# A first round of weights decoded over more steps, and the second token tile's first products put ahead of the first tile's second products

## The chip, the cores and the metric

The kernel runs on one core of one Trainium2 chip. The metric is the device time of one execution in microseconds (us); of several executions the median is taken, and lower is better. Engine names in the rows: PE is the matrix engine, PEld its weight loads, DVE the vector engine, ACT the scalar engine, POOL the GpSimd engine, SP the engine that issues most transfers.

## The reference

What is computed is a sliding-window attention followed by two feed-forward layers, all in float32. Batch is 2, heads 8, sequence 768, head size 64; the model width is 512 and the hidden width 2048, so there are 1536 tokens.

```python
scores = scale * np.matmul(q, k.transpose(0, 1, 3, 2))
keep = is_sink | in_window              # 4 sink keys, window of 128 keys
scores = np.where(keep, scores, -1000000000.0)
a = np.exp(scores - np.max(scores, axis=-1, keepdims=True))
a = a / (np.sum(a, axis=-1, keepdims=True) + 1e-09)
x = np.matmul(a, v)                     # then heads side by side: [1536, 512]
...
h = x @ w_in                            # first layer
g = np.where(h > 0.0, h, np.exp(np.minimum(h, 0.0)) - 1.0)
x = g @ w_out
...
h = x @ w_in2                           # second layer
g = np.maximum(h, 0.0) + alpha * np.minimum(h, 0.0)
out = g @ w_out2
```

## The kernel before, in words

**Numbers.** The layer products are made to float32 accuracy out of a reduced float format: each operand is kept as a high part and a low part, and `matmul3` (L287) makes three matmuls for each pair (high by high, high by low, low by high). A *product* below is one call of `Mlp.g1` or `Mlp.g2`: four pairs, so twelve matmuls. `g1` (L303, tiles `h`) multiplies one 128-row block of the first weight matrix by a tile of tokens; its second half `after` makes the activation `u` and splits it into `gh` (ACT) and `gl` (POOL). `g2` (L341, tiles `o`) multiplies four such blocks by the second weight matrix and adds into `acc`.

**Weights.** They arrive as 64-bit words, in *halves* of 128 by 512: `halves(0)` lists the eight of the first round (four row blocks, each an `io=0` half for `g1` and an `io=1` half for `g2`). `load_w` starts the transfer into one of three `raw` buffers. `decode_w` (L257) takes a half apart: two ACT operations (`wx`, `wq`; L266 and L267), four DVE operations (L269 to L278), an ACT copy to the high part `wh` (L282) and a subtraction for the low part `wl` (L284). It is a generator that stops three times, so that its pieces can be laid between other work. Its scratch tiles come from the pool `wdec`, which lives as long as the kernel. The subtraction runs on DVE, or on the engine passed as `sub`.

**Attention steps.** The attention is cut into 32 units; each has one or two blocks of up to 110 queries for two heads. The units of a token tile are done head pair after head pair: units 0 to 3 give the first 220 tokens, 4 to 7 the next 220, 8 to 15 the next 328 (these units have two blocks and one block in turn), and 16 to 31 the second batch in the same way. The loop over `s` (L610), from 0 to 33, is software-pipelined and its order is written by hand (`manual_schedule`, L597). Step `s` makes the scores of unit `s` (`qk` on PE, L510; mask and minimum on DVE, L518; exponential and its sum on ACT, L523), the values product of unit `s-2` (`x`, L575; its high part `xh` on ACT, its low part `xl` on DVE), the normalisation of unit `s` (`st` on DVE, then `s` on POOL, L540) and the transposes of unit `s-1` (`t` on PE, L554, copied out to `pt`, L638). Each engine executes its own instructions in the order in which they stand.

**Filling.** From step 5 on one product of the first layer's first round is put into each step (`fill`, L588 to L594): for each token tile first its four `g1`, then its four `g2`. When eight or more are due (`FILL_MAX`, L62), a second one is put into the same step. In steps 0 to 4 dummy matmuls (`keep_busy`) stand in the products' place. In steps 0 to 7 one half of the first round is decoded in each step (L625 to L629, L652 to L654); the subtraction of the last four halves is on POOL.

**After the steps.** `mlp_rounds` (L393) does the fifth token tile of the first round, and then all other rounds in tiles of 512 tokens; the halves of the next round are decoded between the products. There the order on each engine is the scheduler's, not written by hand, and it may put an instruction anywhere ahead where its buffers are free. The pools of the attention steps are closed before (`inner.close()`, L669), and the next round's weight pool `wb` takes their memory.

Of the kernel before, what the change touches and what calls it, by code (L numbers as in the profile page):

```python
# [21 lines left out]
P = 128  # L22
# [12 lines left out]
HP = H // 2  # L35
# [19 lines left out]
MS = {2: 0, 3: 1, 4: 5}  # L55
# [6 lines left out]
FILL_MAX = 8  # L62
# [49 lines left out]
def attention_mlp2(  # L112
# [20 lines left out]
    wdec = ctx.enter_context(tc.tile_pool(name="wdec", bufs=2))  # L133
# [123 lines left out]
    def decode_w(pool, m, fc, io, sub=None):  # L257
# [26 lines left out]
        (sub or nc.vector).tensor_tensor(out=wl, in0=xf, in1=wh, op=ALU.subtract)  # L284
# [10 lines left out]
    class Mlp:  # L295
# [3 lines left out]
        def __init__(self, gp, ps):  # L299
            self.gp, self.ps = gp, ps  # L300
            self.g = {}

        def g1(self, m, c0, n, fc):  # L303
# [12 lines left out]
            def after():  # L316
                u = tmp.tile([P, big], F32, tag="u", name=f"u{m}_{t}_{fc}")[:, :n]
                gh = self.gp.tile([P, big], F32R, tag="gh", name=f"gh{m}_{t}_{fc}")[:, :n]
                gl = self.gp.tile([P, big], F32R, tag="gl", name=f"gl{m}_{t}_{fc}")[:, :n]
# [73 lines left out]
    def mlp_rounds(mlp, items, wpools):  # L393
# [22 lines left out]
        def weights_step():  # L416
            j = state["at"]
            if j + 2 < len(order):
                load_w(*order[j + 2][1:])
            done(decode_w(*order[j]))  # L420
            state["at"] = j + 1
# [24 lines left out]
    def distance(blk):  # L446

        rel = relp.tile([P, KW[blk]], I32, tag=f"rel{blk}", name=f"rel{blk}")
# [29 lines left out]
    relp = ctx.enter_context(tc.tile_pool(name="relp", bufs=1))  # L478
    rels = {blk: distance(blk) for blk in MASKS}
# [4 lines left out]
    def fast_path():  # L484
# [4 lines left out]
        ga = inner.enter_context(tc.tile_pool(name="ga", bufs=FG + 1))  # L489
        at = inner.enter_context(tc.tile_pool(name="at", bufs=2))  # L490
        mlp = Mlp(ga, ps)
        soft, trans = {}, {}
        wraw.update(wfirst)

# [96 lines left out]
        for c0, n, t in TOK0[:-1]:  # L591
            at_ = last_of[t * HP + HP - 1] + 2
            fill += [(at_, lambda c0=c0, n=n, fc=fc: mlp.g1(0, c0, n, fc)) for fc in range(FG)]
            fill += [(at_, lambda c0=c0, n=n, d=d: mlp.g2(0, c0, n, 0, d)) for d in range(KC)]  # L594


        order = inner.enter_context(tc.manual_schedule())  # L597
# [3 lines left out]
        for j in range(WPRE, WPRE + 3):  # L601
            load_w(*ws[j])
            if j < HP:
                load_v(j)
        for g in range(HP, HP + LB):
            load_kq(g, at)
            load_v(g, at)
        decodes = {}
        gates = []
        for s in range(nu + 2):  # L610
# [44 lines left out]
            if WPRE <= s and s + 3 < len(ws):  # L655
                load_w(*ws[s + 3])
# [15 lines left out]
        mlp.gp = gb  # L672
        rounds = [(k, t) for k in range(1, 2 * NR) for t in TOK]
        mlp_rounds(mlp, [(0, TOK0[-1])] + rounds, (wa, wb))
        outer.close()

    def general_path():

        with ExitStack() as outer:
            ps = outer.enter_context(tc.tile_pool(name="gps", bufs=4, space=PSUM))  # L680
            wraw.update(wfirst)
            for h in halves(0):
                if h not in wraw:
                    load_w(*h)
                done(decode_w(wa, *h))
# [71 lines left out]
            mlp_rounds(mlp, [(k, t) for k in range(2 * NR) for t in TOK], (wa, wb))  # L757
# [58 lines left out]
```

## Time and profile before

| what | value |
| --- | --- |
| device time, median of 3 runs | 672.32 us (671.1 to 672.47) |
| device time of the profiled execution | 673.24 us |
| its span | 671.1 us |
| PE busy | 642.0 us (96%) |
| DVE busy | 440.8 us (66%) |
| ACT busy | 316.5 us (47%) |
| POOL busy | 207.9 us (31%) |
| mean granted clock of PE | 0.983 of full speed |

The span is the time from the first to the last recorded instruction; the device time has about 2 us more around it. The busy shares are means over the whole span. The attention steps take about the first 180 us of it; the rest is the rounds of the two layers. A timeline row gives the start in us, the length in us, the engine, the source line, the operation, output and input tiles with their sizes, how many instructions were merged, and in brackets the idle time before it on that engine with what ended it.

### The profile page before, as it was taken

How to read it: one execution, taken by the hardware profiler on the slowest of the kernel's cores; microseconds unless marked ns; L12 is line 12 of the kernel's file. 1: busy time of each engine (PE TensorE's matmuls, PEld its weight loads, DVE VectorE, ACT ScalarE, POOL GpSimd, SP SyncE). 2: the span in 40 equal slices, each digit the busy share in tenths (PEclk: the TensorE clock that was granted, in tenths of full speed). 3: DMA queues.
4: the chain of work that ended last, by engine and by line, in shares of the span. 5: the costliest groups of instructions: out<-in, count | busy, mean ns of one | idle time of the engine just before them, and what ended most of it. 6: DMA issues, size and time to landing. Idle time of an engine off the chain costs nothing.

```text
span 671.1 us, 9665 instructions
## 1 busy us (share of the span) xinstructions
PE 642.0 (96%) x3444; PEld 527.0 (79%) x3444; DVE 440.8 (66%) x925; ACT 316.5 (47%) x717; POOL 207.9 (31%) x257
## 2 busy tenths in 40 slices
PE   7966999999999899999999999999999999999996
PEld 6745888888877677888888888888888888888885
DVE  5798566756499997668465876694559673343332
ACT  5676476656478685547445733453524230110010
POOL 2346244534123322133205453332123311331130
PEclk8898899999999999999999999999999999999999
DMA  8665324620044242121112211221111000000112
GB/s 266 169 165 182 106 58 122 170 79 25 1 154 133 91 156 95 49 77 63 63 54 72 64 63 52 75 67 61 63 63 63 32 0 1 1 0 1 63 46 85
DMA packets 21659, 52.87 MB, mean 79 GB/s; under 512 B 2658, under 2 KB 9826, under 8 KB 21602
## 3 DMA queue, kind: packets, MB, share of 16 engines
q1 hardware_dynamic: 21024, 51.93, 24.8%
q8 instruction: 29, 0.48, 0.3%
q10 hardware_dynamic: 578, 0.24, 0.2%
q14 instruction: 28, 0.23, 0.1%
HBM read 49.01 MB, written 3.15 MB: 78 GB/s over the span
## 4 chain that ended last, share of the span: by engine, by line
PE 80%; DVE 11%; ACT 4%; issue 3%; POOL 1%; DMA 1%; ACTq 0%; DVEq 0%; POOLq 0%; SPq 0%
PE o L292 37%; PE h L292 34%; PE x L575 3%; PE t L554 2%; PE qk L510 2%; DVE wx L275 2%; ACT s L523 2%; DVE wl L284 1%; DVE wx L269 1%; DVE wx L278 1%; PE busy L250 1%; DVE u L323 1%; DVE pt L638 1%; DVE wx L272 1%; ACT wx L266 1%
## 5 line engine op out<-in xcount | busy, mean ns | idle before, releaser
L336 POOL TENSOR_TENSOR gl<-u,gh 128x512 fp32r<-128x512 f32 (+3 forms) x104 | 131.5, 1264 | 341.6 <-ACT gh L335 307.2
L292 PE MATMUL o<-gh,wh 128*128 128x512 f32 (+3 forms) x416 | 159.2, 383 | 3.7 <-DVE u L323 2.0
L292 PE MATMUL h<-xh,wh 128*128 128x512 f32 (+3 forms) x416 | 158.9, 382 | 0.0
L292 PE MATMUL o<-gl,wh 128*128 128x512 f32 (+3 forms) x416 | 157.2, 378 | 0.8 <-POOL gl L336 0.8
L292 PE MATMUL h<-xl,wh 128*128 128x512 f32 (+3 forms) x416 | 157.1, 378 | 0.0
L292 PE MATMUL h<-xh,wl 128*128 128x512 f32 (+3 forms) x416 | 156.9, 377 | 0.0
L292 PE MATMUL o<-gh,wl 128*128 128x512 f32 (+3 forms) x416 | 156.5, 377 | 0.0
L335 ACT CAST gh<-u 128x512 fp32r<-128x512 f32 (+3 forms) x104 | 61.0, 586 | 140.9 <-DVE u L331 118.9
L357 DVE TENSOR_TENSOR acc<-o,acc 128x512 f32<-128x512 f32 x72 | 49.4, 688 | 76.9 <-PE o L292 76.9
L292 PEld LDWEIGHTS o<-gh,wh 128*128 128x128 f32 x416 | 78.5, 189 | 23.2 <-DVE u L323 4.1
L292 PEld LDWEIGHTS h<-xh,wh 128*128 128x128 f32 x416 | 78.6, 189 | 17.1 <-DVE u L323 0.3
L292 PEld LDWEIGHTS o<-gl,wh 128*128 128x128 f32 x416 | 78.8, 189 | 15.9 <-POOL gl L336 1.8
L292 PEld LDWEIGHTS h<-xl,wh 128*128 128x128 f32 x416 | 78.7, 189 | 14.6
L292 PEld LDWEIGHTS h<-xh,wl 128*128 128x128 f32 x416 | 78.6, 189 | 14.7
L292 PEld LDWEIGHTS o<-gh,wl 128*128 128x128 f32 x416 | 78.7, 189 | 14.5
L540 POOL TENSOR_SCALAR s<-s,st 110x250 f32<-110x250 f32 (+5 forms) x112 | 52.7, 488 | 86.0 <-DVE st L536 42.6
L282 ACT CAST wh<-wx 128x512 fp32r<-128x512 f32 x64 | 39.5, 619 | 67.7 <-DVE wx L278 29.4
L327 DVE TENSOR_SCALAR u<-h,alpha_sb 128x512 f32<-128x512 f32 x48 | 35.9, 748 | 48.4 <-PE h L292 48.3
L523 ACT ACTIVATE s<-s,st 110x250 f32<-110x250 f32 (+5 forms) x112 | 53.1, 476 | 20.8 <-DVE st L518 20.8
L278 DVE CUSTOM_DVE_ANT_0 wx<-wx,wq 128x1024 uint16<-128x1024 uint16 x64 | 58.0, 906 | 1.3
L284 DVE TENSOR_TENSOR wl<-wx,wh 128x512 fp32r<-128x512 f32 x60 | 45.4, 759 | 17.6 <-PE o L292 9.2
L267 ACT ACTIVATE wq<-wr 128x512 int32<-128x512 uint32 x62 | 41.5, 669 | 32.9 <-DVE wx L278 29.4
(55 smaller groups left out, 664.3 us busy)
## 6 DMA issues: line engine op xcount, KB each, us to landing
wr<-in_w_dram SPq DMA_DIRECT2D x62, 512.0 KB, 3.5
kq<-in_kq_dram SPq DMA_DIRECT2D x16, 237.0 KB, 4.4
vr<-in_vc_dram SPq DMA_DIRECT2D x8, 384.0 KB, 3.7
out_dram<-acc SPq DMA_DIRECT2D x12, 256.0 KB, 2.0
kq<-in_kq_dram SPq DMA_DIRECT2D x16, 180.0 KB, 3.9
vr<-in_vc_dram SPq DMA_DIRECT2D x8, 256.0 KB, 4.0
acc<-in_w_dram SPq DMA_DIRECT2D x2, 512.0 KB, 5.4
kq<-in_kq_dram SPq DMA_DIRECT2D x8, 110.0 KB, 2.7
```

The source lines that it names most:

```text
L267: nc.scalar.activation(r, low.bitcast(U32), AF.Copy, scale=2.0**-29)
L278: nc.vector.tensor_tensor(out=x, in0=x, in1=r, op=ALU.add)
L282: nc.scalar.copy(wh, xf)
L284: (sub or nc.vector).tensor_tensor(out=wl, in0=xf, in1=wh, op=ALU.subtract)
L292: nc.tensor.matmul(out, a, c, start=(i == 0), stop=(i == n - 1))
L327: nc.vector.tensor_scalar(out=u, in0=hp, scalar1=0.0, scalar2=alpha_sb[:, fc : fc + 1], op0=ALU.min, op1=ALU.mult,)
L335: nc.scalar.copy(gh, u)
L336: nc.gpsimd.tensor_tensor(out=gl, in0=u, in1=gh, op=ALU.subtract)
L357: nc.vector.tensor_tensor(out=a, in0=po, in1=a, op=ALU.add)
L523: nc.scalar.activation(sb[:n, j, e, :w], sb[:n, j, e, :w], AF.Exp, bias=st[:n, 0, j, e : e + 1], scale=-1.0, accum_out=st[:n, 1, j, e : e ...
L540: nc.gpsimd.tensor_scalar(out=sb[:n, j, e, :w], in0=sb[:n, j, e, :w], scalar1=st[:n, 3, j, e : e + 1], scalar2=1.0, op0=ALU.mult, op1=ALU. ...
L575: nc.tensor.matmul(px[e * D : e * D + D, o : o + n], vr[:r, vs : vs + D], pt[:r, p0 : p0 + n], start=(k == 0), stop=(k == c - 1),)
```

## The change

The eight halves of the first round are no longer decoded in steps 0 to 7 but in the steps that the list `DS` names (1, 3, 5, 7 for the four `io=0` halves, 9 to 12 for the four `io=1` halves). All subtractions are on DVE. The four `g1` of the second token tile stand ahead of the four `g2` of the first, and the threshold for a second product in a step is 13, which is not reached: each step from 5 to 33 has one product, and the last three products come after the loop. In a step, the copies of the transposes now stand ahead of the normalisation of the step's own unit. The scratch tiles of `decode_w` come from a pool that is closed with the attention steps, and from a new one (`wdec2`) in the freed memory afterwards. The third mask is made in step 2 and not in step 5, and the narrow token tiles have activation buffers of their own.

```diff
-MS = {2: 0, 3: 1, 4: 5}
+MS = {2: 0, 3: 1, 4: 2}
+DS = [1, 3, 5, 7, 9, 10, 11, 12]
-FILL_MAX = 8
+FILL_MAX = 13
...
-    wdec = ctx.enter_context(tc.tile_pool(name="wdec", bufs=2))
...
-        (sub or nc.vector).tensor_tensor(out=wl, in0=xf, in1=wh, op=ALU.subtract)
+        nc.vector.tensor_tensor(out=wl, in0=xf, in1=wh, op=ALU.subtract)
...
+                a, w, bufs = ("n", self.narrow, 2 * FG) if n <= self.narrow else ("", big, None)
...
-        ga = inner.enter_context(tc.tile_pool(name="ga", bufs=FG + 1))
+        ga = inner.enter_context(tc.tile_pool(name="ga", bufs=FG))
+        at2 = inner.enter_context(tc.tile_pool(name="wdec", bufs=2))
...
+        fill += first[0] + first[1] + second[0] + second[1]
+        for a, c in zip(first[2:], second[2:]):
+            fill += a + c
...
-            if s == 0:
-                decodes[0] = decode_w(wa, *ws[0], sub=nc.vector)
-                next(decodes[0])
...
+            if 1 <= s <= nu:
+                for j, (out, in_) in enumerate(transposed(s - 1)):
+                    (nc.scalar.copy if j and s <= DS[HP] else nc.vector.tensor_copy)(out, in_)
             if s < nu:
                 normalised(s)
-            if 1 <= s <= nu:
-                for j, (out, in_) in enumerate(transposed(s - 1)):
-                    (nc.scalar.copy if j and s < len(ws) else nc.vector.tensor_copy)(out, in_)
...
-            if s + 1 < len(ws):
-                decodes[s + 1] = decode_w(wa, *ws[s + 1], sub=nc.vector if s + 1 < FG else nc.gpsimd)
+            if s + 1 in DS:
+                decodes[s + 1] = decode_w(at2, wa, *ws[DS.index(s + 1)])
                 next(decodes[s + 1])
...
+        wdec = outer.enter_context(tc.tile_pool(name="wdec2", bufs=2))
```

What this makes of the order is shown at three places. The numbers behind the names are buffer numbers; in the layers' names the first number is the first token of the tile or the weight block. The first place is DVE in step 7, from the first operation of a decode to the activation `u` of a product. Before:

```order
L269 TENSOR_SCALAR wx_3_1_692<-wx_3_1_692 128x512
L272 TENSOR_SCALAR wx_3_1_692<-wx_3_1_692 128x512
L275 SCALAR_TENSOR_TENSOR wx_3_1_692<-wr_3_1_526,wx_3_1_692 128x512
L269 TENSOR_SCALAR wx_4_0_2399<-wx_4_0_2399 128x512
L278 ISA wx_3_1_692<-wx_3_1_692,wq_3_1_693 128x1024
L533 TENSOR_SCALAR st_708<-st_708 110x4
L272 TENSOR_SCALAR wx_4_0_2399<-wx_4_0_2399 128x512
L536 RECIPROCAL st_708<-st_708 110x4
L275 SCALAR_TENSOR_TENSOR wx_4_0_2399<-wr_4_0_2393,wx_4_0_2399 128x512
L638 COPY pt_2_764<-t_2_759 125x440
L278 ISA wx_4_0_2399<-wx_4_0_2399,wq_4_0_2400 128x1024
L323 SCALAR_TENSOR_TENSOR u_0_2_773<-u_0_2_773,h_0_2_740 128x220
```

The same place with the change, up to the first score of step 8:

```order
L270 TENSOR_SCALAR wx_3_0_638<-wx_3_0_638 128x512
L273 TENSOR_SCALAR wx_3_0_638<-wx_3_0_638 128x512
L276 SCALAR_TENSOR_TENSOR wx_3_0_638<-wr_3_0_187,wx_3_0_638 128x512
L279 ISA wx_3_0_638<-wx_3_0_638,wq_3_0_639 128x1024
L649 COPY pt_2_700<-t_2_695 125x440
L544 TENSOR_SCALAR st_650<-st_650 110x4
L547 RECIPROCAL st_650<-st_650 110x4
L327 SCALAR_TENSOR_TENSOR u_0_2_715<-u_0_2_715,h_0_2_682 128x220
L285 TENSOR_TENSOR wl_3_0_729<-wx_3_0_638,wh_3_0_728 128x512
L529 ISA s_734,st_735<-qk_4_0_736,mask 110x256
```

Before, two decodes run through each other there, the second (`4_0`) being one of the next round that the scheduler put ahead, and the subtraction of `3_1` is not in the list because it is on POOL; with the change there is one decode, its subtraction stands behind `u`, and the copy to `pt` stands ahead of `st`.

The second place is PE in step 9, from a score product to the transposes of unit 8 and what follows them. Before:

```order
L510 MATMUL qk_6_0_864<-kq_611 108x242
L575 MATMUL x_872<-pt_2_843,vr_699 64x110 x4
L575 MATMUL x_872<-pt_3_850,vr_699 64x110 x4
L292 MATMUL o_0_0_0_883<-gh_0_0_600,wh_0_1_531 128x220
...
L554 MATMUL t_4_900<-ident,s_790 128x110 x4
L554 MATMUL t_5_907<-ident,s_790 125x110 x4
L292 MATMUL o_0_0_1_915<-gh_0_0_600,wh_0_1_531 128x220
```

The same place with the change:

```order
L521 MATMUL qk_6_0_812<-kq_561 108x242
L586 MATMUL x_820<-pt_2_781,vr_645 64x110 x4
L586 MATMUL x_820<-pt_3_788,vr_645 64x110 x4
L293 MATMUL h_220_0_835<-xh,wh_0_0_299 128x220
...
L565 MATMUL t_4_848<-ident,s_734 128x110 x4
L565 MATMUL t_5_855<-ident,s_734 125x110 x4
L521 MATMUL qk_4_0_891<-kq_642 110x256
```

A `g2` of the first tile with a second one behind the transposes has become a single `g1` of the second tile (`h_220_0`), behind which the next step's scores stand.

The third place is DVE at the end of the attention steps, from the copy of the last transposes on. Before:

```order
L638 COPY pt_6_2374<-t_6_2369 121x432
L585 TENSOR_TENSOR xl<-x_2377,xh 128x108
L284 TENSOR_TENSOR wl_4_0_2408<-wx_4_0_2399,wh_4_0_2407 128x512
L284 TENSOR_TENSOR wl_5_0_2435<-wx_5_0_2426,wh_5_0_2434 128x512
L269 TENSOR_SCALAR wx_6_0_2461<-wx_6_0_2461 128x512
L272 TENSOR_SCALAR wx_6_0_2461<-wx_6_0_2461 128x512
L269 TENSOR_SCALAR wx_7_0_2496<-wx_7_0_2496 128x512
L275 SCALAR_TENSOR_TENSOR wx_6_0_2461<-wr_6_0_2397,wx_6_0_2461 128x512
L323 SCALAR_TENSOR_TENSOR u_1208_0_2451<-u_1208_0_2451,h_1208_0_2411 128x328
```

The same place with the change:

```order
L649 COPY pt_6_2305<-t_6_2300 121x432
L327 SCALAR_TENSOR_TENSOR u_768_3_2307<-u_768_3_2307,h_768_3_2287 128x440
L596 TENSOR_TENSOR xl<-x_2315,xh 128x108
L270 TENSOR_SCALAR wx_4_0_2397<-wx_4_0_2397 128x512
L273 TENSOR_SCALAR wx_4_0_2397<-wx_4_0_2397 128x512
L276 SCALAR_TENSOR_TENSOR wx_4_0_2397<-wr_4_0_2391,wx_4_0_2397 128x512
L270 TENSOR_SCALAR wx_5_0_2424<-wx_5_0_2424 128x512
L279 ISA wx_4_0_2397<-wx_4_0_2397,wq_4_0_2398 128x1024
L273 TENSOR_SCALAR wx_5_0_2424<-wx_5_0_2424 128x512
L327 SCALAR_TENSOR_TENSOR u_1208_0_2449<-u_1208_0_2449,h_1208_0_2409 128x328
L285 TENSOR_TENSOR wl_4_0_2406<-wx_4_0_2397,wh_4_0_2405 128x512
```

The first two decodes of the next round (`4_0`, `5_0`), of which only the subtractions were left here before, now stand here from their first operation on.

## Rows read from the trace of the kernel before

**Rows 1.** windows by stage, the header line and one line each

```profile
core 0: us, PE busy (x) PEld busy (x) DVE busy (x) ACT busy (x) POOL busy (x), PEclk, DMA share, GB/s
...
0.00:36.72 36.72, 30.09 (x220) 25.37 (x220) 26.16 (x100) 23.42 (x68) 11.68 (x44) 0.86 0.72 207
...
36.72:68.11 31.39, 20.30 (x175) 16.77 (x173) 27.39 (x75) 21.89 (x67) 17.49 (x27) 0.88 0.64 187
...
68.11:98.40 30.29, 29.75 (x270) 25.38 (x268) 17.83 (x72) 17.09 (x63) 11.97 (x25) 0.95 0.28 75
...
180.00:256.00 76.00, 71.80 (x331) 57.69 (x331) 73.94 (x114) 58.71 (x109) 20.79 (x16) 1.00 0.37 124
```

**Rows 2.** timeline of DVE (start, length, us): first score of steps 0-2, 5-9, 13

```profile
6.71 0.27 DVE L518 CUSTOM_DVE_ANT_0 s<-qk,mask 110x110 f32<-110x110 f32 x1 [0.39 <-PE qk L510]
...
13.27 0.26 DVE L518 CUSTOM_DVE_ANT_0 s<-qk,mask 110x110 f32<-110x110 f32 x1
...
18.22 0.27 DVE L518 CUSTOM_DVE_ANT_0 s<-qk,mask 110x110 f32<-110x110 f32 x1
...
35.80 0.41 DVE L518 CUSTOM_DVE_ANT_0 s<-qk,mask 110x250 f32<-110x250 f32 x1
...
45.21 0.41 DVE L518 CUSTOM_DVE_ANT_0 s<-qk,mask 110x250 f32<-110x250 f32 x1
...
50.63 0.41 DVE L518 CUSTOM_DVE_ANT_0 s<-qk,mask 110x250 f32<-110x250 f32 x1
...
58.88 0.41 DVE L518 CUSTOM_DVE_ANT_0 s<-qk,mask 110x256 f32<-110x256 f32 x1
...
67.12 0.40 DVE L518 CUSTOM_DVE_ANT_0 s<-qk,mask 108x242 f32<-108x242 f32 x1
...
86.83 0.40 DVE L518 CUSTOM_DVE_ANT_0 s<-qk,mask 108x242 f32<-108x242 f32 x1
```

**Rows 3.** timeline of ACT, the end of step 0's exponentials

```profile
8.68 0.19 ACT L523 ACTIVATION_READ_ACCUMULATOR s<-s,st 110x1 f32 x1
```

**Rows 4.** timeline of DVE, step 6, from its remainder to the decode's end

```profile
47.00 0.39 DVE L585 TENSOR_TENSOR xl<-x,xh 128x220 fp32r<-128x220 f32 x1 [0.38 <-ACT xh L583]
47.30 0.42 DVE L269 TENSOR_SCALAR wx<-wx 128x512 f32<-128x512 f32 x1
...
49.55 0.16 DVE L533 TENSOR_SCALAR st<-st 110x4 f32<-110x4 f32 x1
```

**Rows 5.** timeline of DVE, two operations that ran long in steps 5 and 6

```profile
37.90 1.26 DVE L269 TENSOR_SCALAR wx<-wx 128x512 f32<-128x512 f32 x1
...
42.67 2.61 DVE L463 SCALAR_TENSOR_TENSOR mask<-skey,lims,mask 128x6 f32<-128x6 int32 x1
```

**Rows 6.** timeline of POOL, weight subtractions and normalisations, contended and not

```profile
44.00 1.26 POOL L284 TENSOR_TENSOR wl<-wx,wh 128x512 fp32r<-128x512 f32 x1
...
63.04 3.12 POOL L540 TENSOR_SCALAR s<-s,st 110x256 f32<-110x256 f32 x4 [0.86 <-ACT wx L266]
...
77.28 1.84 POOL L540 TENSOR_SCALAR s<-s,st 110x256 f32<-110x256 f32 x4 [6.62 <-ACT acc L355]
```

**Rows 7.** timeline of DVE, round 1's first decode and first two subtractions

```profile
55.18 0.42 DVE L269 TENSOR_SCALAR wx<-wx 128x512 f32<-128x512 f32 x1
...
180.55 1.29 DVE L284 TENSOR_TENSOR wl<-wx,wh 128x512 fp32r<-128x512 f32 x2 [0.47 <-ACT wh L282]
```

**Rows 8.** timeline of PE, the values product of step 9 and the wait before it

```profile
66.39 1.79 PE L575 MATMUL x<-pt,vr 125*64 125x110 f32 x16 [4.52 <-DVE pt L638]
```

**Rows 9.** chain that ended last, in order of time: start, us, one product each

```profile
68.18 2.83 PE o L292 x12
...
79.66 1.53 PE h L292 x12
```

**Rows 10.** windows of 2 us around the same wait, with the granted clock

```profile
66.00:68.00 2.00, 1.61 (x16) 1.45 (x16) 1.86 (x7) 1.55 (x5) 0.46 (x2) 0.50 0.79 293
...
70.00:72.00 2.00, 2.00 (x16) 2.00 (x16) 0.49 (x1) 0.34 (x1) 0.67 (x2) 0.74 0.52 164
```

More of the change, by code (lines that the diff above doesn't have):

```diff
@@ L300, in __init__ @@
             self.gp, self.ps = gp, ps
-            self.g = {}
+            self.g, self.narrow = {}, 0
         def g1(self, m, c0, n, fc):
@@ L317, in after @@
                 u = tmp.tile([P, big], F32, tag="u", name=f"u{m}_{t}_{fc}")[:, :n]
-                gh = self.gp.tile([P, big], F32R, tag="gh", name=f"gh{m}_{t}_{fc}")[:, :n]
-                gl = self.gp.tile([P, big], F32R, tag="gl", name=f"gl{m}_{t}_{fc}")[:, :n]
+                a, w, bufs = ("n", self.narrow, 2 * FG) if n <= self.narrow else ("", big, None)
+                gh, gl = (
+                    self.gp.tile([P, w], F32R, tag=f"g{c}{a}", name=f"g{c}{m}_{t}_{fc}", bufs=bufs)[:, :n]
+                    for c in "hl"
+                )
                 if m == 0:
@@ L419, in weights_step @@
                 load_w(*order[j + 2][1:])
-            done(decode_w(*order[j]))
+            done(decode_w(wdec, *order[j]))
             state["at"] = j + 1
@@ L444, in attention_mlp2, with distance @@
     masks = {}
-    def distance(blk):
-        rel = relp.tile([P, KW[blk]], I32, tag=f"rel{blk}", name=f"rel{blk}")
+    def distance(blk, pool=None):
+        if pool:
+            rel = pool.tile([P, 4 * QB], F32, tag="pt", name=f"rel{blk}", bufs=PB).bitcast(I32)
+        else:
+            o = HP * (2 * KTOT[0] + VCH[0] * 2 * D) + WPRE * 2 * DM + sum(KW[i] for i in MASKS if i < blk)
+            rel = room[:, o : o + KW[blk]].bitcast(I32)
+        rel = rel[:, : KW[blk]]
         for c, n, k in mask_runs(blk):
@@ L488, in fast_path @@
         inner = ExitStack()
[L489 removed]
+        ga = inner.enter_context(tc.tile_pool(name="ga", bufs=FG))
         at = inner.enter_context(tc.tile_pool(name="at", bufs=2))
+        at2 = inner.enter_context(tc.tile_pool(name="wdec", bufs=2))
         mlp = Mlp(ga, ps)
+        mlp.narrow = TOK0[0][1]
         soft, trans = {}, {}
         wraw.update(wfirst)
+        rels.update({blk: distance(blk, at) for blk in MASKS[3:]})
         def scores(i):
@@ L590, in fast_path @@
         fill = []
-        for c0, n, t in TOK0[:-1]:
+        first, second = [], []
+        for j, (c0, n, t) in enumerate(TOK0[:-1]):
             at_ = last_of[t * HP + HP - 1] + 2
-            fill += [(at_, lambda c0=c0, n=n, fc=fc: mlp.g1(0, c0, n, fc)) for fc in range(FG)]
-            fill += [(at_, lambda c0=c0, n=n, d=d: mlp.g2(0, c0, n, 0, d)) for d in range(KC)]
-        order = inner.enter_context(tc.manual_schedule())
+            first.append([(at_, lambda c0=c0, n=n, fc=fc: mlp.g1(0, c0, n, fc)) for fc in range(FG)])
+            second.append([(at_, lambda c0=c0, n=n, d=d: mlp.g2(0, c0, n, 0, d)) for d in range(KC)])
+        fill += first[0] + first[1] + second[0] + second[1]
+        for a, c in zip(first[2:], second[2:]):
+            fill += a + c
+        inner.enter_context(tc.manual_schedule())
         make_mask(0)
@@ L600, in fast_path @@
         ws = halves(0)
-        for j in range(WPRE, WPRE + 3):
+        for j in range(WPRE, HP):
             load_w(*ws[j])
-            if j < HP:
-                load_v(j)
+            load_v(j)
         for g in range(HP, HP + LB):
@@ L684, in general_path @@
                     load_w(*h)
-                done(decode_w(wa, *h))
+                done(decode_w(wdec, wa, *h))
             nqt = S // P
@@ L756, in general_path @@
             mlp = Mlp(gb, ps)
-            mlp_rounds(mlp, [(k, t) for k in range(2 * NR) for t in TOK], (wa, wb))
+            mlp_rounds(mlp, [(k, t) for k in range(2 * NR) for t in TOK], (wa, wb), wdec)
     fast = nc.values_load(flag_i[0:1, 0:1], min_val=0, max_val=1)
```

17 lines of the change are left out of this document (9 added, 8 removed).

## The prediction

> **What bounds the kernel now.** I read the windows by stage first, since the share of PE over the whole span hides where it waits. PE is idle for 6.6 us of the first 36.7 and for 11.1 of the next 31.4 (36.72 less 30.09, 31.39 less 20.30), but for only 0.5 us of the 30.3 after that; DVE is busy for 27.4 of the 31.4 us in which PE waits most [rows 1]. So up to about 68 us the steps go at the pace of DVE and what feeds it, and from there at the pace of PE. A second stage in which PE loses time lies behind the attention steps: 4.2 us idle in 180 to 256 us, with DVE busy for 73.9 of 76 [rows 1].
>
> Next come the step lengths, read on DVE from one step's first score to the next one's [rows 2]. Steps 0 and 1 take 6.56 and 4.95 us; steps 0 to 4 together 29.09 (6.71 to 35.80). Steps 5, 6, 7 and 8, which hold one product each, take 9.41, 5.42, 8.25 and 8.24, together 31.32. Steps 9 to 12 take 19.71 (67.12 to 86.83) and hold six products, since in two of them a second one is due. Step 6 is the clean one: from the start of the decode to its end 2.25 us (47.30 to 49.55) [rows 4], and nothing else in the way. What makes 5, 7 and 8 longer stands in three views. Two operations of DVE run long: one of the decode 1.26 us where in step 6 it takes 0.42, and a mask of six columns 2.61 us [rows 4, 5]; in the second POOL's weight subtraction of 1.26 us runs [rows 6]. At 55.18 us DVE begins a decode that belongs to the next round [rows 7], by the order on DVE one of two that stand in steps 7 and 8. And in step 9 PE has waited 4.52 us for the transposes' copy and then runs slow: its values product takes 1.79 us [rows 8], its next product 2.83 where a later one takes 1.53 [rows 9], at a granted clock of 0.50, the lower level of 1.2 GHz, and back at the upper one shortly before 72 us [rows 10].
>
> **The change part by part.** All sums are made against the profiled execution (span 671.1 us, 673.24 with what lies around it); the median of the runs is 672.32, about 1 us below, and I take the difference over to it.
>
> *Steps 0 to 4.* The decodes of steps 0, 2 and 4 leave. Step 0 ends its exponentials at 8.87 us (8.68 plus 0.19) [rows 3], 2.16 after its first score; with the sum's reciprocal and a mask behind it (0.9 by estimate, from a decoded step's remainder below) that is 3.1. A decoded step without a product is step 1 of before, 4.95; 5.2 for each of steps 1 and 3, since the copy now waits for the decode. Without the decode (4.95 less 2.25) 2.7 are left, and with the wait for the exponentials 3.2 for each of steps 2 and 4. Sum: 3.1 + 2 x 5.2 + 2 x 3.2 = 19.9 for 29.09, a gain of 9.2.
>
> *Steps 5 to 8.* Steps 5 and 7 decode, 6 and 8 do not. A decoded step with a product is step 6 of before, 5.42, plus the subtraction that comes over from POOL, 0.65 on DVE (1.29 for two) [rows 7]; that is 6.1, and 6.5 with room for the low part that the first product waits for. A step without a decode goes at PE's pace: in 68.11 to 98.40 us PE works through seven steps in 30.3 us [rows 1], 4.3 each at 1.3 products, so 4.2. Sum: 2 x 6.5 + 2 x 4.2 = 21.4 for 31.32, a gain of 9.9. In it is that no subtraction on POOL and no decode of the next round is left in these steps, as the order on DVE shows.
>
> *Steps 9 to 12.* All four decode now: 4 x 6.5 = 26.0 for 19.71, a loss of 6.3. They hold four products where six stood, and the two that are left over are done when PE sets the pace: 2 x 1.53 [rows 9] = 3.1 more. The first `g2` of the first tile needs the last decode, whose subtraction stands right ahead of step 13's scores; only its last matmul reads it, so nothing is added.
>
> So far 9.2 + 9.9 - 6.3 - 3.1 = 9.7 us gained. Three things take from it.
>
> *PE's clock.* In steps 9 to 12 PE has some 3.5 us of work in 6.5 (a step's 4.3 with fewer products) and so waits over 2 us in each. Before, the clock fell after 4.52 us without work and PE ran about 5 us at the lower level behind it (66.4 to 71.5) [rows 8, 10], which costs half of it, 2.5 us. Bounds: nothing, if the gaps are too short; 2.5 plus the rival below, if it stays low. I take 2.5, the nearest row.
>
> *The moved instructions that now meet on POOL.* The activations' low parts stay on POOL and the six decoded steps hold one each. The nearest row for a meeting is the 1.26 against 0.42 [rows 4, 5], 0.84; six of them 5.0, none at all 0. They stand at a step's head, beside the scores rather than the decode, so I take 1.3, near the lower end.
>
> *The end of the attention steps.* The next round's first two decodes lose their early place and come to DVE's busiest stage, 180 to 256 us. Each is 2.25 plus 0.65. On the path whole, they cost 5.8; hidden, 0. I take 0.4: the order on DVE has six whole decodes between the start of the last token tile and the first activation of the next round, before as after (before 6_0 to 7_1, with the change 4_0 to 5_1); from there to the end of that round DVE is two decodes behind at every product, but not later, and makes them up at the end, where PE has buffers ahead. What is queued behind them is the activation of that tile, for which PE's products wait. The three products behind the loop cover the last steps' waits; the transfers go ahead as before, in three raw buffers, and no queue of SP has a transfer behind one that it needs earlier.
>
> Edits at nothing: the mask moved to step 2 (in the 3.2), the narrow buffers, the copies ahead of the normalisation (POOL has a product's time before PE needs its result; if that cover is gone, some 0.3 us in a step with a one-block unit ahead).
>
> Net: 9.7 - 2.5 - 1.3 - 0.4 = 5.5 us gained; 672.3 - 5.5 = 666.8.
>
> **The rivals.** *More is left* (663.0): the clock holds and nothing meets on POOL, a gain of 9.3. For it: gaps of 2 us are half of the 4.52. Against: they come in a row.
>
> *The clock stays low in steps 9 to 12* (669.8). Then PE's own chain of a step, values 1.79, product 2.83, transposes about 1.6 and the copy about 1.0, is 7.2 us and longer than 6.5; four steps lose 0.75 each, 3.0 together. For it: PE at half its clock is busy nearly all of such a step, which before brought the clock back.
>
> *The two decodes come to the path* (672.2). 5.8 in place of 0.4. For it: DVE's 73.9 of 76 us [rows 1]. Against: the order there.
>
> *DVE and POOL keep each other waiting* (675.1, slower). Of POOL the same kind of normalisation, four instructions, takes 3.12 us with decoding beside it and 1.84 without [rows 6]. With the change each decoded step has a decode, a subtraction and a normalisation again, so these six steps could stay as long as steps 7 and 8 were, 8.25, in place of 6.5: 6 x 1.75 = 10.5, of which the 1.3 and about 0.9 of the clock term are counted already, so 8.3 more. It decides from 0.9 us in each of the six steps. Against: step 6, which had POOL's normalisation and a decode and took 5.42. The Trainium skill, in "SBUF — State Buffer", section "SBUF: two separate sides", says that DVE and GpSimd share a pair of ports as an exclusive lock, and that a DVE operation with two SBUF inputs takes it against a GpSimd operation that reads SBUF. That speaks against moving the subtraction to DVE, as it would hold up the normalisation there; the two lengths of the normalisation agree with it, but no row shows the wait on PE's path.
>
> *The change does not do what it says*: the order on the engines shows that it does; left at 2%.
>
> **How the numbers follow.** Forecast 46%, more left 15%, low clock 14%, two decodes 11%, mutual waiting 12%, not as said 2%. The predicted time is the forecast's. The range leaves out mutual waiting and little of the rest: from 661.5 (the gain of 9.3 and 1.5 for the estimated remainders) to 672.5 (the two decodes on the path). A measurement of this kernel can tell about 0.2% (1.3 us) from no change: faster are the first three and a few per cent of partly exposed decodes, 77%; the same most of the two decodes, 10%; slower 13%.
>
> **What would show it.** Right: the first score of step 5 on DVE near 27 us, of step 9 near 48, of step 13 near 74 (before 35.80, 67.12, 86.83); no decode of the next round before the end of the attention steps; PE idle in the 76 us behind that end still 4 to 5 us. Wrong: step 13 after 80 us; steps 9 to 12 longer than 7.4 us each; a granted clock of 0.5 for most of them; or PE idle 9 us and more behind the end of the steps, with DVE as what it waits for. What would make the forecast wrong on the good side is PE clocked high through steps 9 to 12 and the last three products hiding more than they cost.

## The result, and the profile after

The changed kernel takes 660.76 us (median of 659.56 to 662.34), the kernel before beside it 672.39; the ratio is 0.983, with an interval of 0.980 to 0.986. The forecast was 666.8 with a range from 661.5: the time lies just below the range, and the move of 11.6 us is twice the 5.5 that the sum gave. The experiments show that the sum had the size of what it spoke of, and that as much again came from a place it did not speak of.

First the attention steps of the changed kernel, in the timeline of DVE: the first score of steps 5, 9 and 13. They answer to [rows 2], which has 35.80, 67.12 and 86.83 there.

```profile
27.64 0.42 DVE L529 CUSTOM_DVE_ANT_0 s<-qk,mask 110x250 f32<-110x250 f32 x1 [0.45 <-PE qk L521]
...
50.14 0.40 DVE L529 CUSTOM_DVE_ANT_0 s<-qk,mask 108x242 f32<-108x242 f32 x1
...
76.49 0.40 DVE L529 CUSTOM_DVE_ANT_0 s<-qk,mask 108x242 f32<-108x242 f32 x1
```

The windows of the changed kernel by stage; the first three are steps 0 to 4 (with the start), 5 to 8 and 9 to 12, and they answer to [rows 1].

```profile
core 0: us, PE busy (x) PEld busy (x) DVE busy (x) ACT busy (x) POOL busy (x), PEclk, DMA share, GB/s
0.00:27.64 27.64, 25.25 (x208) 21.31 (x208) 18.55 (x84) 16.95 (x56) 10.36 (x42) 1.00 0.86 240
27.64:50.14 22.50, 20.00 (x189) 16.68 (x186) 17.03 (x62) 17.77 (x58) 10.88 (x21) 0.92 0.59 159
50.14:76.49 26.35, 18.53 (x145) 15.14 (x145) 21.71 (x67) 18.15 (x54) 9.05 (x16) 0.85 0.43 129
...
174.65:250.65 76.00, 70.89 (x337) 58.71 (x337) 74.06 (x116) 59.66 (x111) 22.13 (x16) 1.00 0.41 132
...
191.34:265.00 73.66, 68.88 (x298) 55.03 (x297) 68.47 (x107) 52.52 (x93) 18.77 (x13) 1.00 0.41 132
...
270.00:650.00 380.00, 380.00 (x1679) 314.63 (x1678) 236.12 (x351) 138.70 (x236) 109.91 (x82) 1.00 0.15 50
```

A mark parts the attention from what follows: the first matmul of round 1, the first that is 512 wide. It starts here at 191.34 us.

```profile
191.34 0.39 PE L293 MATMUL h<-xh,wh 128*128 128x512 f32 x1
```

In the kernel before, the same timeline of PE has it at 196.59.

```profile
196.59 0.40 PE L292 MATMUL h<-xh,wh 128*128 128x512 f32 x1
```

Up to the mark the change gains 5.25 us, from it to the end of the span 474.51 (671.1 less 196.59) less 469.16 (660.5 less 191.34), 5.35 more. In that second part PE waits longer than before, not shorter: idle for 4.78 us of 191.34 to 265, and for 2.73 of the like stretch of the kernel before:

```profile
196.59:270.00 73.41, 70.68 (x301) 55.40 (x300) 66.59 (x102) 52.50 (x94) 19.75 (x14) 1.00 0.36 121
```

So PE must do the same 2,016 matmuls faster. From 270 to 650 us it is busy without a gap in both kernels, at full clock. The kernel before, the same window:

```profile
270.00:650.00 380.00, 380.00 (x1651) 309.49 (x1650) 233.88 (x347) 140.11 (x238) 110.84 (x82) 1.00 0.14 47
```

1,651 matmuls in 380 us where the changed kernel has 1,679. The chain of waits shows which. It merges products of one kind (start, us, engine, tile, line, count); in the kernel before, groups of 48 take either 11.20 or 10.91 us:

```profile
289.62 11.20 PE o L292 x48
300.82 10.92 PE h L292 x48
311.74 11.20 PE o L292 x48
...
367.44 11.20 PE h L292 x48
378.64 10.91 PE o L292 x48
```

In the changed kernel all of them take 10.88:

```profile
274.32 10.88 PE h L293 x48
285.20 10.88 PE o L293 x48
...
350.49 10.88 PE o L293 x48
361.37 10.88 PE h L293 x48
```

By 48, that is 233.3 ns from start to start in the long groups of the kernel before, 227.3 in its others, and 226.7 in the changed kernel. The first three rows of before are from an even round, and its `o` products are slow; the last two are from an odd one, and there it is the `h` products. The weights of even rounds lie in pool `wa`, those of odd rounds in `wb`; `h` products stream `xh` and `xl`, `o` products `gh` and `gl` of pool `gb`. The start addresses of these tiles in a partition, taken from the two built kernels and given by what they leave when divided by 256, and below them the time from start to start in ns:

```
                    before         after
xh, xl, wa          224            224
wb, gb              0              224
h, even (wa, x)     alike  227.3   alike  226.7
o, even (wa, gb)    differ 233.3   alike  226.7
h, odd  (wb, x)     differ 233.3   alike  226.7
o, odd  (wb, gb)    alike  227.3   alike  226.7
```

The shift has one line of the change as its source, which the diff of the change above leaves out: the pool of the masks' distances, which lay between `tmp` and the pools that hold `wb` and `gb`, is dissolved, and its 4,384 bytes (17 times 256 and 32) are gone from ahead of them.

```diff
-    relp = ctx.enter_context(tc.tile_pool(name="relp", bufs=1))
```

`wdec` left that stretch too, but `wdec2` came back to it in the same size of 8,192.

### The profile page after: what moved, and what is told of

Same layout as the page of the kernel before. It is cut to its first block, busy times and chain, and to the rows that moved or that the text cites. A ratio compares the mean times of both kernels' runs of the same rounds, so it can differ in the third digit from the quotient of the medians.

```text
span 660.5 us, 9670 instructions
## 1 busy us (share of the span) xinstructions
PE 633.7 (96%) x3444; PEld 526.6 (80%) x3444; DVE 435.9 (66%) x927; ACT 315.7 (48%) x719; POOL 204.4 (31%) x253
## 4 chain that ended last, share of the span: by engine, by line
PE 78%; DVE 13%; ACT 4%; issue 2%; POOL 1%; DMA 1%; DVEq 0%; ACTq 0%; SPq 0%; POOLq 0%
PE o L293 36%; PE h L293 34%; PE x L586 3%; DVE wx L276 3%; DVE wx L279 2%; ACT s L534 2%; PE t L565 2%; PE qk L521 2%; DVE wl L285 2%; DVE wx L273 1%; DVE wx L270 1%; DVE pt L649 1%; DVE u L327 1%; DVE acc L361 1%; PE busy L251 1%
## 5 line engine op out<-in xcount | busy, mean ns | idle before, releaser
L340 POOL TENSOR_TENSOR gl<-u,gh 128x512 fp32r<-128x512 f32 (+3 forms) x104 | 133.1, 1280 | 327.6 <-ACT gh L339 322.5
L293 PE MATMUL o<-gh,wh 128*128 128x512 f32 (+3 forms) x416 | 157.3, 380 | 5.5 <-DVE u L327 5.5
L276 DVE SCALAR_TENSOR_TENSOR wx<-wr,wx 128x512 int32<-128x512 int32 x62 | 56.6, 914 | 1.0
L285 DVE TENSOR_TENSOR wl<-wx,wh 128x512 fp32r<-128x512 f32 x64 | 46.8, 733 | 15.5 <-ACT wh L283 13.9
```

Of the source, the lines that this page charges most:

```text
L276: nc.vector.scalar_tensor_tensor(out=x, in0=high, scalar=-0x40000000, in1=x, op0=ALU.bitwise_and, op1=ALU.bitwise_or)
L285: nc.vector.tensor_tensor(out=wl, in0=xf, in1=wh, op=ALU.subtract)
L293: nc.tensor.matmul(out, a, c, start=(i == 0), stop=(i == n - 1))
L340: nc.gpsimd.tensor_tensor(out=gl, in0=u, in1=gh, op=ALU.subtract)
```

## Experiments: where the tiles lie

Theory PLACE: the spacing of the rounds' matmuls hangs on how the start of the weights and the start of the streamed tile stand to each other. Rival ORDER: it comes with the order of work. An unused tile moves `wb` and `gb` and changes nothing else. In the kernel before:

```diff
+        pada = outer.enter_context(tc.tile_pool(name="pada", bufs=1))
+        pada.tile([P, 440], F32, tag="pada", name="pada_0")
         wb = outer.enter_context(tc.tile_pool(name="wb", bufs=FG))
```

> The kernel before, with one unused tile of 1,760 bytes per partition put in front of the weight tiles of the odd rounds (pool wb) and the tiles gh and gl (pool gb) behind them, and nothing else. In the kernel before the tiles xh, xl and the weights of pool wa all start at addresses that leave 1,248 when divided by 2,048, those of wb and gb at 1,536; with the unused tile all start at 1,248, as in the changed kernel. Theory PLACE (the 128x512 products of the rounds are issued 233.3 ns apart where the weights and the moving tile start differently, 226.7 ns where they start alike): the h products of odd rounds and the o products of even rounds, some 990 matmuls, go from 233.3 to 226.7 ns, 6.6 us less, so about 665.8 us; the first product of round 1 starts near 196.6 us as before. Rival ORDER (the closer spacing comes with the changed order of work or the moved decode temporaries): no change, 672.4 us, and the spacing stays at 233.3 ns in these products.

Measured: 665.14 us beside 671.78, ratio 0.991 (0.989 to 0.993). This is 6.6 us for a tile that nothing reads. The window and two groups of the chain:

```profile
270.00:650.00 380.00, 380.00 (x1678) 314.78 (x1677) 235.53 (x350) 138.58 (x235) 109.46 (x81) 1.00 0.15 49
...
309.34 10.88 PE o L292 x48
...
363.74 10.88 PE h L292 x48
```

1,678 (1,679 in the changed kernel), and no long group is left. Its attention is still the slow one: round 1 begins at 194.60. That this is 2.0 us ahead of the kernel before, with the same order of work, comes from step 2, which took 7.31 us there and 5.34 here. In the one execution PE had the lower clock in that step, in the other the upper one; the same window, first of the kernel before, then of b_same:

```profile
18.20:23.20 5.00, 5.00 (x32) 4.73 (x31) 4.16 (x17) 2.62 (x11) 1.32 (x4) 0.50 1.07 256
```

```profile
18.20:23.20 5.00, 4.21 (x44) 3.53 (x42) 4.48 (x17) 4.20 (x13) 1.65 (x4) 1.00 1.08 255
```

So two executions can lie 2 us apart in the attention by the clock alone. Now the other way round, in the changed kernel, with 288 bytes:

```diff
+        pada.tile([P, 72], F32, tag="pada", name="pada_0")
         wb = outer.enter_context(tc.tile_pool(name="wb", bufs=FG))
```

> The changed kernel, with one unused tile of 288 bytes per partition in front of the pools wb and gb, so that their tiles start at 1,536 modulo 2,048 as in the kernel before, and xh, xl and wa stay at 1,248. Theory PLACE: the h products of odd rounds and the o products of even rounds are issued 233.3 ns apart again, the others 226.7; 6.6 us more than the changed kernel, about 667.4 us, which is what the order of work alone is worth; the attention and the start of round 1 (191.3 us) do not move. Rival ORDER: 660.8 us and 226.7 ns throughout.

Measured: 666.63 us beside 671.78, ratio 0.992 (0.990 to 0.994).

```profile
270.00:650.00 380.00, 380.00 (x1651) 309.46 (x1650) 233.56 (x347) 137.97 (x234) 109.40 (x81) 1.00 0.15 48
...
305.61 11.20 PE o L293 x48
...
361.31 11.20 PE h L293 x48
```

The 1,651 of before are back, in the same products, and round 1 begins at 190.01. PLACE holds in both directions and ORDER falls. The change splits into two parts that add up: all of it but the place, called the order of work below, is worth 671.78 less 666.63, 5.15 us, and the place alone 6.64; together 11.8, and the whole change measured 11.6.

What is meant by alike? Three kernels with two unused tiles each (ahead of `wb`, and between `wb` and `gb`) give three differences apiece.

> The changed kernel with an unused tile of 64 bytes per partition in front of pool wb and one of 128 bytes between wb and gb. The starts of weights and moving tile then differ by 64 bytes in the h products of odd rounds, by 128 in the o products of odd rounds, by 192 in the o products of even rounds, by 0 in the h products of even rounds. PLACE with a unit of 64 bytes (288 is not a multiple of it): all stay at 226.7 ns, 660.8 us. PLACE with any difference counting, or with a unit of 128 or 256 or more: some or all of the three kinds at 233.3 ns, up to 1,556 matmuls, 10.4 us more, 671.2 us.

Measured: 669.46 us beside 671.78, ratio 0.996 (0.994 to 0.997).

```profile
270.00:650.00 380.00, 380.00 (x1642) 307.57 (x1641) 234.12 (x348) 138.62 (x235) 110.04 (x81) 1.00 0.15 48
```

The lowest count of all. 64, 128 and 192 are all slow (233.4, 232.4 and 233.3 ns on the mean from 270 us on), so a unit of 64 or 128 falls.

> The changed kernel with an unused tile of 32 bytes per partition in front of pool wb and one of 512 bytes between wb and gb. The starts of weights and moving tile differ by 32 bytes in the h products of odd rounds, by 512 in the o products of odd rounds, by 544 in the o products of even rounds. PLACE with a unit of 64 bytes: the first and the third at 233.3 ns, the second at 226.7, about 667.4 us. With any difference counting: all three at 233.3 ns, 671.2 us. With a unit of 32 bytes or less (then 288 would not be slow either): 660.8 us.

Measured: 666.85 us beside 671.78, ratio 0.992 (0.990 to 0.994), and 1,651 matmuls in the window. The `h` products of odd rounds (32) and the `o` products of even ones (544) are slow, the `o` products of odd ones (512) are not.

> The changed kernel with an unused tile of 256 bytes per partition in front of pool wb and one of 1,024 bytes between wb and gb. The starts of weights and moving tile differ by 256 bytes in the h products of odd rounds, by 1,024 in the o products of odd rounds, by 1,280 in the o products of even rounds. So far 0 and 512 were fast, 32, 64, 128, 192, 288 and 544 slow. With a unit of 512 bytes: the first and third at 233.3 ns, the second at 226.7, about 667.4 us. With a unit of 256 bytes: all at 226.7 ns, 660.8 us.

Measured: 661.04 us beside 671.11, ratio 0.985 (0.984 to 0.987).

```profile
270.00:650.00 380.00, 380.00 (x1678) 314.63 (x1678) 234.25 (x348) 137.10 (x233) 108.19 (x80) 1.00 0.15 51
```

Nothing is slow at 256, 1,024 and 1,280. The unit is 256 bytes: of the differences tried, 0, 256, 512, 1,024 and 1,280 are fast, 32, 64, 128, 192, 288 and 544 slow, and how far a slow one is off made no odds. The changed kernel, run again beside this one, took 661.4 us, ratio 0.985 (0.983 to 0.987), as expected:

> The changed kernel once more, beside the next one on the same chip: 660.8 us as before, within its spread of 659.6 to 662.3, and 226.7 ns between the products of the rounds.

The last of the kind moves `wl` of the odd rounds alone, inside a wider tile:

```diff
-        wl = pool.tile([P, DM], F32R, tag=f"wl{io}", name=f"wl{nm}")
+        o = 72 if fc // FG % 2 else 0
+        wl = pool.tile([P, DM + (P if o else 0)], F32R, tag=f"wl{io}", name=f"wl{nm}")[:, o : o + DM]
```

> The changed kernel in which the low parts of the weights of the odd rounds (wl in pool wb) are put 288 bytes further on inside a wider tile, so that they alone start differently from the moving tiles; wh and all moving tiles start alike. Each product is a row of matmuls (xh by wh, xl by wh, xh by wl). If a matmul is late because its own weights start differently from its own moving tile, one in three of the odd rounds' matmuls, the one after which the next wh follows or the one before, is 6.7 ns longer: 1,124 matmuls by a third, 2.5 us, about 663.3 us. If one odd pair in a product slows every matmul of it, 7.5 us, about 668.3 us. If only the high parts matter: 660.8 us.

Measured: 667.37 us beside 671.11, ratio 0.994 (0.992 to 0.996); that is near the 668.3 of the second case. One weight tile in three out of place costs as much as all. Within a product the delay is uneven: in the odd rounds the next matmul starts 233 ns behind `xh` by `wh`, 239 behind `xl` by `wh` and 228 behind `xh` by `wl` (medians of the starts), where the changed kernel has 227 three times. The weight loads stand one matmul ahead; here is one (PEld), and the matmul that starts with it:

```profile
319.98 0.19 PEld L294 LDWEIGHTS h<-xh,wl 128*128 128x128 f32 x1
```

```profile
319.98 0.40 PE L294 MATMUL h<-xl,wh 128*128 128x512 f32 x1
```

So the matmul that suffers most is not the one that uses the displaced `wl` but the one beside which `wl` is loaded. That speaks for, and does not show, a collision between the load of the next weights and the tile that is being streamed; why the matmul ahead of it is 6 ns late as well stays open.

## Experiments: the order of work

Here the places are the changed kernel's, so the comparison is with its 660.8 us. First the spreading of the decodes is taken back:

```diff
-DS = [1, 3, 5, 7, 9, 10, 11, 12]
+DS = [1, 2, 3, 4, 5, 6, 7, 8]
...
```

> The changed kernel with its eight decodes in eight steps on end (1 to 8) in place of 1, 3, 5, 7, 9, 10, 11, 12; the order of the products, the pools and the places of all tiles are the changed kernel's. By the step costs of the prediction (5.2 us for a decoded step without a product, 6.5 with one, 3.2 and 4.2 without a decode): steps 0 to 4 take 4.0 us more, 5 to 8 take 4.6 more (first score of step 5 near 31.6, of step 9 near 58.7), 9 to 12 take 9.2 less (step 13 near 75.9); in all 0.6 us less than the changed kernel, about 660.2 us. Rival SPREAD (a decode in every step costs more than the same decode with a step between, and the spreading carries the gain): step 13 after 81 us and the time 666 us or more.

Measured: 658.95 us (657.07 to 660.84) beside 671.59, ratio 0.980 (0.978 to 0.982). The first scores of steps 5, 9 and 13:

```profile
31.72 0.41 DVE L529 CUSTOM_DVE_ANT_0 s<-qk,mask 110x250 f32<-110x250 f32 x1
...
59.84 0.40 DVE L529 CUSTOM_DVE_ANT_0 s<-qk,mask 108x242 f32<-108x242 f32 x1
...
77.38 0.40 DVE L529 CUSTOM_DVE_ANT_0 s<-qk,mask 108x242 f32<-108x242 f32 x1
```

The step costs gave 31.6, 58.7 and 75.9. SPREAD falls: step 13 begins at 77.38 and not after 81, and the spreading that gives the change its name gains nothing. (Steps 5 to 8 take 7.03 us each on the mean here, the changed kernel's six decoded steps with a product 6.5, so a neighbour with a decode may cost something.) This kernel has the lowest median of all; its interval and that of the changed kernel (0.980 to 0.986) meet, that of the changed kernel's second measurement (0.983 to 0.987) lies above it, and they did not run side by side, so that it is faster is likely and not shown.

> The kernel of a_steps with the order of the products undone too: first and second products of a tile behind each other, and a second product in a step from 8 waiting ones on, as before the change. Against a_steps it shows what the product order is worth by itself. By the prediction the products of the first two tiles keep PE as busy in either order: the same within 1 us (about 660.2 us). Rival PRODUCT ORDER: the first o products wait for the last decode's weights, and PE idles 2 us or more between 55 and 75 us, so 662 us or more.

With the order of the products undone too (and a threshold of 8): 661.25 us (659.46 to 661.4), ratio 0.984 (0.982 to 0.986). That is 2.3 us above a_steps by the medians, but the two intervals just meet, and in the profiled executions round 1 begins at 189.85 us against 190.84 in a_steps, earlier and not later. Whether the product order is worth anything stays open.

A kernel without both still gains, so most of the gain of the order of work lies in the rest of the change. Step lengths of before against this kernel: step 0 6.56 and 3.05 us (its decode is gone), step 5 9.41 and 7.28 (the mask is gone), step 7 8.25 and 7.40, step 8 8.24 and 6.09 (the next round's decodes are gone from both); steps 1, 3, 4 and 6 are 0.0 to 0.8 longer, and step 2, 7.31 and 5.69, took 5.34 in b_same with the order of before. These lengths point to parts; they don't show what each is worth by itself. One of the parts is tried by itself: the subtractions of the second half back on POOL.

```diff
+                decodes[s + 1] = decode_w(at2, wa, *ws[DS.index(s + 1)], sub=nc.vector if s + 1 < DS[FG] else nc.gpsimd)
...
```

> The changed kernel with the subtractions of the second half of the weights (wl of the four decodes in steps 9 to 12) on POOL, as the kernel before had them. By the prediction a meeting of such a subtraction on POOL with DVE's decode costs 0.84 us where the subtraction on DVE costs 0.65: within 1 us of the changed kernel, 660 to 662 us. Rival MEETING (the long operations of DVE in the kernel before come from the subtraction on POOL, and they hold up the step): steps 9 to 12 longer by 1 us or more each, 664 us or more, and single DVE operations of the decode of 1.2 us in place of 0.4.

Measured: 662.45 us (659.73 to 664.45), ratio 0.985 (0.983 to 0.988). The interval meets that of the changed kernel. In the profile steps 9 to 12 take 25.41 us against 26.35, and round 1 begins at 191.41 against 191.34. A long operation of the kind that MEETING named is there once, where its like in the other three steps takes 0.43 us:

```profile
65.11 1.37 DVE L273 TENSOR_SCALAR wx<-wx 128x512 int32<-128x512 int32 x1
```

It runs beside POOL's subtraction:

```profile
64.75 1.45 POOL L285 TENSOR_TENSOR wl<-wx,wh 128x512 fp32r<-128x512 f32 x1
```

But the four steps together are no longer for it: MEETING falls as a cost, and which engine subtracts is worth less than can be seen.

Another part: the scratch tiles in a pool that lasts the whole kernel.

```diff
+    wdec = ctx.enter_context(tc.tile_pool(name="wdec", bufs=2))
...
-        at2 = inner.enter_context(tc.tile_pool(name="wdec", bufs=2))
...
-        wdec = outer.enter_context(tc.tile_pool(name="wdec2", bufs=2))
...
```

> The changed kernel with the decode's temporaries in one pool that lasts the whole kernel, as before the change; all other tiles stay where they are. The first two decodes of the next round can then go early: by the order on DVE they stand in steps 12 and 13 and no longer behind the attention. In the changed kernel PE waits 4.8 us for DVE between 191 and 265 us, in the kernel before 2.7 in the like stretch: if the two decodes behind the attention cost that difference, 2.0 us are saved there; in steps 12 and 13 they cost between 0 (PE sets the pace) and 5.8 (both whole on the path). By the prediction (0.4 for the two decodes behind the attention, steps at DVE's pace until 12): about 2 us slower than the changed kernel, 662.8 us. Rival HIDDEN: about 659 us.

Measured: 663.79 us, ratio 0.988 (0.986 to 0.990), 3.0 more than the changed kernel by the medians and 1.1 by the spans of the profiled executions. Step 12 takes 7.48 us in place of 6.06, and step 13 stays at 5.56. Behind the attention nothing comes back. What PE waits for there (185 to 270 us; total, times, longest), with the early decodes:

```profile
PE o L294 <- DVE u L328: 5.7, 5, 2.5
PE o L294 <- POOL gl L341: 0.8, 2, 0.4
```

In the changed kernel, the waits of 190 to 672 us:

```profile
PE o L293 <- DVE u L327: 4.8, 6, 1.5
```

So the two decodes behind the attention are not what PE waits for there. Keeping them out of the steps is worth 1 to 3 us by these numbers, which is not shown: the intervals of the two kernels meet. A last kernel puts the question once more, with both decodes begun where PE sets the pace:

```diff
+            if s in (25, 28):
+                begun.append(decode_w(wdec, later, *halves(1)[len(begun)]))
+                next(begun[-1])
+            if s in (26, 29):
+                next(begun[-1])
...
```

> The kernel of a_steps (decodes in steps 1 to 8, the changed kernel's product order and places) in which the next round's first two decodes are begun in steps 25 to 29, where PE sets the pace and DVE is busy for 19.6 of 32.8 us in the changed kernel; only the rounding to the high part and the subtraction stay behind the attention. In a_steps PE waits 3.8 us for DVE between 185 and 270 us. If these waits come from the two decodes behind the attention and steps 25 to 29 hide 4.5 us on DVE: about 2 us less than a_steps, 657 us. Rival BEHIND: DVE's backlog there comes from the other six decodes, or the two are late in the steps where they now stand: the same as a_steps or up to 4 us slower, 659 to 663 us.

Measured: 661.8 us beside 671.11, ratio 0.987 (0.985 to 0.989); the changed kernel beside it had 0.985. BEHIND holds: PE still waits 3.8 us for `u`, as in a_steps, and the steps where the decodes now stand get longer (step 26 7.02 us against 4.32 in a_steps, step 29 8.59 against 5.28; the two between are 1.6 us shorter together).

## Why the prediction was right and wrong

**The step that failed is the sum's silence on the rounds.** It ends with the three leftover products and the stage behind the attention, and the 470 us behind them stand in it at no change. There the change took 6.6 us. *Edits at nothing* names the narrow buffers and the copies, but not where the edited pools put the tiles behind them. The trace of before held the sign, in its rows of 11.20 and 10.91 us: two lengths for the same 48 matmuls, at one clock and with no wait. Had their cause been known, 666.8 less 6.6 would have been 660.2.

**The order of work was right in its size.** Alone it gains 5.15 us (ratio 0.990 to 0.994) where 5.5 was forecast. Its terms:

| term | forecast | measured in the profile |
| --- | --- | --- |
| steps 0 to 4 | 19.9 | 20.67 (27.64 less 6.97) |
| steps 5 to 8 | 21.4 | 22.50 |
| steps 9 to 12 | 26.0 | 26.35 |
| step 13 begins | near 74 | 76.49 |
| from step 13 to round 1, against before | 3.1 | 114.85 for 109.76, 5.1 more |
| cost of the lower clock | 2.5 in steps 9 to 12 | about 3.6, in steps 8 and 13 |
| PE idle in 76 us behind the attention | 4 to 5 | 5.11 |

The early terms are 0.8, 1.1 and 0.4 us too hopeful. The sum's sign for step 13, near 74, leaves out the 3.8 us that the sum takes off these steps for the clock and POOL; with them it would be near 78, and step 13 came at 76.49. Behind step 13 more was lost than the 3.1 of the three products. These errors have both signs and cancel in part, and 2.0 of the 29.09 us for steps 0 to 4 were the clock of one execution (step 2 in b_same); that the net came within 0.4 us is partly luck. a_steps shows that the costs of a step carry over, within 1.5 us at step 13, to an order that was not yet run.

*PE's clock.* In steps 5 to 13 the waits came and the clock fell three times, and the cost lies in other steps than the sum said. The timeline of PE in the changed kernel, three values products and the waits ahead of them:

```profile
43.50 1.03 PE L586 MATMUL x<-pt,vr 125*64 125x110 f32 x16 [2.01 <-DVE pt L649]
...
62.67 0.99 PE L586 MATMUL x<-pt,vr 121*64 121x108 f32 x8 [3.51 <-DVE pt L649]
...
75.45 0.99 PE L586 MATMUL x<-pt,vr 121*64 121x108 f32 x8 [2.66 <-DVE pt L649]
```

And the clock behind them (windows; the column PEclk is the third from the end):

```profile
44.00:48.00 4.00, 4.00 (x29) 3.86 (x25) 2.36 (x11) 2.68 (x10) 2.92 (x5) 0.57 1.01 289
...
62.00:66.00 4.00, 3.33 (x19) 3.07 (x20) 3.02 (x12) 2.32 (x8) 2.90 (x5) 0.50 0.78 215
...
76.49:82.10 5.61, 5.61 (x26) 5.16 (x28) 2.48 (x10) 1.54 (x6) 2.53 (x6) 0.50 0.39 115
```

0.50 is the lower level, 1.2 GHz. The first stretch falls into step 8, where PE is busy without a gap; the step took 5.61 us. In a_256_1024 the same wait, 2.00 us, stands ahead of that step, PE stays at the upper level, and the step took 4.25:

```profile
42.71 1.03 PE L586 MATMUL x<-pt,vr 125*64 125x110 f32 x16 [2.00 <-DVE pt L649]
```

```profile
44.00:48.00 4.00, 4.00 (x44) 3.39 (x43) 2.75 (x14) 3.77 (x13) 3.01 (x7) 1.00 1.03 265
```

That is 1.4 us, which covers the 1.1 us by which steps 5 to 8 missed their term. In the second stretch DVE sets the pace and the term costs nothing that steps 9 to 12 show (26.35 us; a_256_1024, where the clock fell at another place of these steps, has 26.33). The third is step 13, with PE again without a gap; in a_steps it does the same products at the upper level in 3.36 us:

```profile
77.38:80.74 3.36, 3.36 (x30) 2.85 (x28) 2.34 (x11) 1.84 (x7) 2.35 (x5) 1.00 0.45 126
```

That is 2.25 us more; with the 3.1 of the three products it makes 5.35, near the 5.1 us measured behind step 13. So the clock's term of 2.5 us measured about 3.6.

*DVE and POOL.* 1.3 us was put in for meetings, and a rival of 8.3 beside it. The six decoded steps with a product (5, 7 and 9 to 12) take 39.1 us together, and 6.5 each without any meeting would be 39.0, so neither is seen; with four subtractions back on POOL steps 9 to 12 did not get longer either (25.41 and 26.35). The Trainium skill, "SBUF — State Buffer", section "SBUF: two separate sides", has the pair of ports that the two engines share as an exclusive lock, which one instruction holds to its end. The decode operation of 1.37 us in a_pool agrees with it; on the path of the changed kernel no run shows a loss from it.

*The end of the attention.* 0.4 for two decodes: PE's idle time there rose by 2.05 us (4.78 and 2.73), but a_long and a_begun show that waits of this size stay when the decodes are elsewhere. A part of the rise goes with the place: 74 us from the mark on, first b_same (idle for 3.47 us), then a_288 (3.63):

```profile
194.60:268.60 74.00, 70.53 (x303) 55.89 (x302) 66.64 (x102) 53.13 (x95) 19.94 (x15) 1.00 0.37 121
```

```profile
190.01:264.01 74.00, 70.37 (x301) 55.75 (x300) 69.11 (x108) 52.47 (x94) 18.88 (x13) 1.00 0.42 132
```

So the place alone adds 0.7 us of waiting and the order alone 0.9, where 0.4 stood. That DVE catches up with the two decodes by the end of that round, as the prediction had it, is neither contradicted nor shown; what the waits do come from is open.

**The rivals.** "More is left" comes closest in time (663.0) and for the wrong reason: the clock did not hold. The clock that stays low, the two decodes and the mutual waiting would all have been slower than a_288, and none came.

## What to carry to other kernels

Before costing a reordering, see whether the change adds, removes or resizes a pool: every tile behind it moves, and a stage that the edit does not touch can change its speed. When equal instructions stand in one trace with two lengths, at one clock and with no wait, compare where their operands lie before taking either length as given. And where an edit has a name, cost its parts apart: here the spreading gained nothing and the product order nothing that could be shown, while 4,384 bytes gained 6.6 us.

## What the runs showed of the hardware

128x512 matmuls of these operands (float32 values kept as reduced floats), on end at the full clock, start 226.7 ns apart when the weights and the streamed tile have starts that differ by a multiple of 256 bytes in their partition, and 233.3 ns apart when they do not (2.9% more). The differences tried are five on the multiple and six off it. For a whole group of 48 no third length came up: 10.88 to 10.92 us on it, 11.14 to 11.20 off it. It was tried on this width and this format alone. The Trainium skill, "TensorE: Matmul & The Clock Gate", section "Step-by-step: what each phase is for", gives TensorE two independent read ports, one for the streamed operand and one for the weights, so that loading the next weights takes no read bandwidth from the running matmul; by that the place of one to the other would not matter, and b_same and a_288 show that it does.

The same wait of 2.0 us at the same place in the program was followed by the lower clock in the changed kernel and by the upper one in a_256_1024, and the step behind it took 5.61 and 4.25 us. Two kernels whose PE does the same work in the attention can so differ by the clock alone, and a step length from one profile is best checked in a second.
